# A fused attention and two-MoE kernel: the first MoE2 weight splits let go one per step, row-list merges queued later, and eight softplus copies moved to ScalarE

## The chip, the cores and the metric

The kernel runs on one core of a Trainium2 chip. The metric is the device time of one execution in microseconds (us). Five engines run side by side, each through its own list of instructions in order: TensorE (PE in the rows; PEld is its weight load), VectorE (DVE), ScalarE (ACT), GpSimd (POOL) and SyncE (SP), which issues most DMAs. An instruction that waits holds up everything behind it on its engine. TensorE's granted clock has two levels here, 1.2 and 2.4 GHz; in the rows it stands as a share of the full level (PEclk).

## What is computed

```python
attn_out = _attn_ref(q, k, v)                  # 4 x 8 heads, 576 tokens, window 128, head_dim 64
x = attn_out.transpose(0, 2, 1, 3).reshape(2304, 512)
# MoE1: one dense block with a softplus between
h = x @ w_in                                   # 512 -> 2048
g = np.maximum(h, 0.0) + np.log1p(np.exp(-np.abs(h)))
x = g @ w_out                                  # 2048 -> 512
# MoE2: 8 experts, the best two for each token
noisy_logits = x @ w_gate + np.log1p(np.exp(x @ w_noise)) * noise
top2 = np.argpartition(-noisy_logits, 2, axis=1)[:, :2]
top2_w = softmax(noisy_logits at top2)
for e in range(8):
    for k in range(2):
        mask = top2[:, k] == e
        h = np.maximum(x[mask] @ w1[e], 0.0)
        out[mask] += top2_w[mask, k, None] * (h @ w2[e])
```

## The kernel before

The 2304 tokens are cut into 9 chunks of 256 (`NCH`). Three stages follow each other and overlap at their borders.

**Attention** fills the first chunks. **MoE1** runs as a list of 144 jobs (`jobs`, `NT` = 144); job t is a chunk c and one sixteenth fc of the hidden width. The loop at the end of the kernel does, for each t: `mm1(t)`, the up matmuls of job t (12 matmuls into a PSUM buffer `h`), some side work, `mm2(t - 3)`, the down matmuls of the job three steps before (6 matmuls into `y`), and some side work again. There are two `h` buffers, so `mm1(t)` can only start when VectorE has read the `h` of job t - 2. I call the last jobs NT-8 to NT-1, and one turn of this loop a step.

Between `mm1` and `mm2` a job passes through the softplus chain: ScalarE takes Abs, Exp and Ln (L584 to L586, tiles `sa`, `sl`), VectorE takes `su` (L592) and `sl` (L587, the one that reads `h` and lets its buffer go), GpSimd adds a rounding correction in halves of 128 columns (L559, `su` and `sl`), and then `gh`, a rounded copy, is made (ScalarE L589 for the first six sixteenths of a chunk, VectorE L590 for the others) and `gl`, the rest (VectorE L591).

When a chunk of MoE1 is complete, `route(c)` is fed into the side work, one item in each half step: transposes of the chunk (L679 evacuates them, `x1T`), the logits (L687), `r_sum` and `r_top2` (the small VectorE operations of L723), then `r_rank(c)`, whose TensorE matmuls need `r_mb`, the mask of the chosen experts, and which ends with four indirect DMAs of GpSimd (L790) that write token records into lists by expert (`rect`). Behind the last chunk comes `late_table`, whose matmul needs `mcum`, the running count.

**MoE2** works on groups of 256 or 128 list entries. For each group SyncE reads the four record lists (`rk`, L1074); `merge` (VectorE, L1085 and L1088) folds them into `rc`; GpSimd then gathers the rows (L1102, `xg`); TensorE transposes them, and `xh`, `xl` are made (L1120, L1121). Groups 0 to 3 are known early (an early table made from the first six chunks), so group 0 is merged and gathered while MoE1 still runs.

The MoE2 weights come as tiles of 128 x 1024 (0.5 MB): `w2_load` issues the load on SyncE, into four tiles of their own (`raw` in the rows) or into the ring of 24 weight tiles (`rawp`), and `w2_split` queues the split, `whi` on ScalarE (L1212) and `wlo` on VectorE (L1210), which lets a `raw` tile go. At most `NSPLIT` = 5 split tiles stand ahead of their use. In the kernel before no split is queued until the flag `splitting` is set at t == NT - 4; then `pump` queues all five.

The order on each engine is made by the class `Order`, when the program is built: each operation has an estimated cost, `chain(..., after=x)` puts a chain of operations into a heap x us of planned time from now, and the operations are written out in the order of their planned start. The numbers in the plan set the order alone; on the chip semaphores set the time.

Of the kernel before, what the change touches and what calls it, by code (L numbers as in the profile page):

```python
# [14 lines left out]
AF = mybir.ActivationFunctionType  # L15
# [8 lines left out]
class Order:  # L24
# [11 lines left out]
    def chain(self, *steps, after=0.0):  # L36

        heapq.heappush(self.heap, (self.now + after, self.count, steps, 0))
        self.count += 1
# [54 lines left out]
def ca(n):  # L94
    return 0.16 + n * 0.00083
# [15 lines left out]
def moe_chain_kernel(ctx, tc, qk, v, w_in, w_out, w_gate, w_noise, noise, w1, w2, out):  # L111
# [6 lines left out]
    NF = w_in.shape[0]  # L118
# [442 lines left out]
    def mm1(t):  # L561
        c, fc = divmod(t, NF)
        if c == 0:
            weights(2 * fc)
        if fc == 0:
            u = attn_last(c)
            for hp in range(4):
                need(("c", 4 * u + hp))
            for z, x in enumerate(XT[c]):
                dma(lambda z=z, x=x: SP.dma_start(xspill[c, z], f32(x).rearrange("p k t -> p (k t)")),  # L570
                    ("xo", c, z), 1 << 19)
        if fc == NA:
            for z in range(2):
                need(("xi", c, z))
            if c + 1 < NCH:
                x_load(c + 1)
        w = W[2 * fc]
        ph = up(lambda z, kc: w[:, z, kc * P:(kc + 1) * P], XT[c], CT, ("hr", t))
        a = tl(mid, [P, CT], F32, "sa", 2, ("g", t))
        u = tl(mid, [P, CT], F32, "su", 3, ("g", t))  # L580
        l = tl(mid, [P, CT], F32, "sl", 3, ("g", t))
        gh = tl(mid, [P, CT], F32R, "gh", 4, ("mm2", t))
        gl = tl(mid, [P, CT], F32R, "gl", 4, ("mm2", t))
        chain(("A", ca(CT), lambda: ACT.activation(a, ph, AF.Abs)),  # L584
              ("A", ca(CT), lambda: ACT.activation(a, a, AF.Exp, scale=-1.0), ("e", t)),
              ("A", ca(CT), lambda: ACT.activation(l, a, AF.Ln, bias=1.0)),  # L586
              ("V", cv(CT), lambda: DVE.scalar_tensor_tensor(l, ph, 0.0, l, op0=OP.max, op1=OP.add), ("hr", t)),  # L587
              ("P", cg(CT), lambda: by_halves(l, l, u, OP.add), None, (("d", t),)),
              ("A", ca(CT), lambda: ACT.activation(gh, l, AF.Copy)) if fc < NA else  # L589
              ("V", cv2(CT), lambda: DVE.tensor_copy(gh, l)),  # L590
              ("V", cv(CT), lambda: DVE.tensor_sub(gl, l, f32(gh)), ("g", t)))  # L591
        chain(("V", cv2(CT), lambda: DVE.tensor_scalar(u, a, 1.0, 1.0, op0=OP.add, op1=OP.subtract), None, (("e", t),)),  # L592
              ("P", cg(CT), lambda: by_halves(u, a, u, OP.subtract), ("d", t)), after=2 * ca(CT) + 0.15)
        if fc == NA - 1:
            for z in range(2):
                emitted(("xo", c, z))
            mark(("mm1", c))
        if fc == NF - 1:
            mark(("mm1b", c))
        G[t] = (gh, gl)  # L600
# [195 lines left out]
    def route(c):  # L796
        for _ in range(3):
            yield None
        yield lambda: r_transpose(c, 0)
        yield lambda: r_transpose(c, 1)  # L800
        if c + 1 < NCH:
            yield lambda: part_load(c + 1)
        yield lambda: r_logits(c)
        yield None
        yield None
        yield lambda: r_sum(c)
        for _ in range(6):
            yield None
        yield lambda: r_rank(c)
        if c == NCH - 1:  # L810
            yield None
            yield lambda: late_table(c)

    nconv, nfreed, nback = [0], [0], [0]
# [246 lines left out]
    def g_rows(g):  # L1061

        n, eo, i = groups[g]
        eo = TB[eo]
        rc = tl(p2, [P, 2, 2], I32, "rc", 6, ("gdone", g))
        rk = tl(p2, [P, NCOPY, 2, 2], I32, "rk", 6, ("rows", g))
        GR[g] = dict(rc=rc)
        ps = pieces(g)
        r0 = {}

        def read(k, i, dst, m):
            if i not in r0:
                r0[i] = SP.value_load(eo[0:1, 1, i:i + 1], min_val=0, max_val=E * T)
            SP.dma_start(dst, rect[k][bass.ds(r0[i], dst.shape[1] * m), :].rearrange("(a p) z -> p a z", p=m))  # L1074

        for i, sl in ps:
            m = sl.stop - sl.start
            for k in range(NCOPY):
                reads.append((g, lambda k=k, i=i, sl=sl, m=m: read(k, i, rk[sl, k, :n, :], m)))
                if sl.start:  # L1080
                    reads.append((g, lambda k=k, i=i, m=m: read(k, i, rk[:m, k, 1:2, :], m)))

        def merge():

            DVE.tensor_reduce(rc[:, :n, 0], rk[:, :, :n, 0].rearrange("p k a -> p a k"), axis=AX.X, op=OP.min)  # L1085
            if n == 1:
                DVE.tensor_reduce(rc[:P // 2, 1:, 0], rk[:P // 2, :, 1:, 0].rearrange("p k a -> p a k"), axis=AX.X, op=OP.min)
            DVE.tensor_reduce(f32(rc[:, :n, 1]), f32(rk[:, :, :n, 1]).rearrange("p k a -> p a k"), axis=AX.X, op=OP.add)  # L1088
        def last():
            chain(("V", 0.4, merge, ("rows", g)), after=6.0)  # L1090
            if g < 3 or g - 3 in turned:
                g_start(g)
            GR[g]["read"] = True
        reads.append((g, last))
# [38 lines left out]
    REG, W2, RAW2 = {}, {}, {}  # L1133
    NSPLIT = 5
    NXTRA = 4
    splitting = [False]
    extra, inring, nsplit = set(), [0], [0]

    def ring_left():
# [59 lines left out]
    def w2_split():  # L1199
        skip_singles()  # L1200
        j = wsp[0]
        if j >= wl[0] or not splitting[0] or nsplit[0] >= NSPLIT or nback[0] < len(sidx) or ring_left() < 2:
            return False
        wsp[0] += 1
        nsplit[0] += 1
        t = RAW2[j]
        hi, lo = W2[j] = [wpool.tile([P, 1024], F32R, name=x, tag="w", bufs=NRING) for x in ("whi", "wlo")]

        def low():
            DVE.tensor_sub(lo, t, f32(hi))  # L1210
            w2_drop(j)
        chain(("A", ca(1024), lambda: ACT.activation(hi, t, AF.Copy), None, (("r2", j),)),  # L1212
              ("V", cv(1024), low, ("w2", j)))
        return True
# [216 lines left out]
    for t in range(NT + max(L2, len(items) + 2)):  # L1431
        if t == 4:
            SP.dma_start(wgn[:, :, :E], w_gate.rearrange("(c p) e -> p c e", p=P))
            SP.dma_start(wgn[:, :, E:2 * E], w_noise.rearrange("(c p) e -> p c e", p=P))
            SP.dma_start(nz, noise.rearrange("(a p) e -> p a e", p=P))
        if t == 20:
            prepare1()
        if t > 40 and t % 2:
            p = next(zfeed, None)
            if p is not None:  # L1440
                p()
        due[0] = min(NSL, 2 * NA + max(0, t - 2 * NA + 2) // 2)
        if t in starts:
            c, n = starts[t]
            if feed is not None:
                for p in feed:
                    p()
            feed = pieces_of(c) if c + 1 < NCH else None
            total = 2 * (attn_until(c + 1) - attn_until(c)) if feed else 0
            fed, gap, gaps = 0, 0, 2 * n - 2  # L1450
        if t == last_start - (NF - NA):
            open_p2()
        if t == last_start - (NF - NA) + 2:
            early_table(NCH - 4)
        if t == last_start:
            few_t()
        if t == NT - 4:
            splitting[0] = True
            pump()
        if t < NT:  # L1460
            c, fc = jobs[t]
            if c == NCH - 1 and fc == 1:
                x_load(0)
            mm1(c * NF + fc)
            if c == 0 and fc == NA + 3:
                part_load(0)
            used(2 * fc, c)
            if NT - 3 < t:
                if t == NT - 2:
                    read_rows(0)  # L1470
                    need(("gl", 0))
                g_transpose(0, t - NT + 2)
                if t == NT - 1:
                    turned.add(0)
                    if "read" in GR.get(3, ()):
                        g_start(3)
        else:
            phase2(t - NT)
        side_work()
        if 0 <= t - L2 < NT:  # L1480
            c, fc = jobs[t - L2]
            mm2(c * NF + fc)
            used(2 * fc + 1, c)
            if fc == NA - 1:
                part_evac(c)
            if fc == NF - 1:
                y_evac(c)
                rfeed = chained(rfeed, route(c))
        if 0 <= t - NT - 2 < len(items):
            s3(*items[t - NT - 2])  # L1490
        side_work()
# [65 lines left out]
```

## Time and profile before

| | us |
|---|---|
| median of 3 runs | 1101.99 |
| the profiled execution | 1101.02 |
| its span, first to last instruction | 1098.9 |
| TensorE matmul busy | 1040.1 (95%) |
| VectorE busy | 703.8 (64%) |
| ScalarE busy | 608.2 (55%) |
| GpSimd busy | 582.4 (53%) |

TensorE is busy nearly all the time, and its shares hide two kinds of lost time: where it is idle, and where it is busy at the lower clock. The change lies around the border of MoE1 and MoE2, from about 573 to 660 us of the span, so what matters is read from that stretch.

### The profile page before, as it was taken

What the parts mean: (1) busy time and instruction counts of PE and PEld (TensorE: products, weight loads), DVE (VectorE), ACT (ScalarE), POOL (GpSimd) and SP (SyncE); (2) the same over time, 40 slices, a digit from 0 to 9 for tenths busy, and PEclk for the clock granted to TensorE, in tenths of its full rate; (3) what the DMA queues carried; (4) which work ended last, traced back from release to release, by engine and by line L of the source; (5) the groups of instructions that cost most, each with busy time, mean ns of one, the idle gap of its engine ahead of it and who ended that gap; (6) DMA issues with size and microseconds to landing.
All of it is one profiled execution on the core that took longest, in us unless ns stands there. A gap on an engine that the chain in (4) does not pass through costs nothing.

```text
span 1098.9 us, 21433 instructions
## 1 busy us (share of the span) xinstructions
PE 1040.1 (95%) x7045; PEld 881.7 (80%) x7045; DVE 703.8 (64%) x1910; ACT 608.2 (55%) x1447; POOL 582.4 (53%) x935
## 2 busy tenths in 40 slices
PE   5699999999999999999988899999999999999995
PEld 3577777777789888888877789999996999689964
DVE  7965778888764666666766577665553655365531
ACT  7976778888664444444435345555543554355431
POOL 4776779989786677777766233332222231323111
PEclk8899999999999999999999899999999999999998
DMA  7331453565683322122238759878889987897742
GB/s 296 133 117 50 167 195 130 191 231 170 196 311 119 123 78 77 42 75 78 87 105 257 275 139 253 261 216 214 229 224 330 315 231 219 314 325 233 204 116 31
DMA packets 97317, 202.13 MB, mean 184 GB/s; under 512 B 34160, under 2 KB 44912, under 8 KB 97200
## 3 DMA queue, kind: packets, MB, share of 16 engines
q1 hardware_dynamic: 87264, 180.21, 49.4%
q0 software_dynamic: 9936, 20.49, 9.4%
q8 instruction: 58, 0.95, 0.4%
q14 instruction: 59, 0.48, 0.2%
HBM read 161.49 MB, written 39.17 MB: 183 GB/s over the span
## 4 chain that ended last, share of the span: by engine, by line
PE 66%; DVE 3%; POOL 3%; DMA 3%; ACT 2%; issue 2%; SPq 1%; DVEq 0%; POOLq 0%; ACTq 0%
PE h L189 30%; PE y L189 19%; PE z L189 10%; PE t L200 3%; DMA rk<-rect 2%; PE h L1281 2%; PE y L1331 1%; PE t L189 1%; POOL sl L559 1%; POOL su L559 1%; PE z L1331 1%; PE t L342 1%; DMA out<-ys,rc 1%; POOL s L375 1%; DVE wlo L1210 0%
## 5 line engine op out<-in xcount | busy, mean ns | idle before, releaser
L189 PE MATMUL h<-xh,w 128*128 128x256 f32 x1152 | 240.5, 292 | 8.4 <-DVE sl L587 8.4
L1344 POOL DMA_INDIRECT out<-ys,rc x42 | 82.6, 1967 | 275.4 <-DVE ys L1354 116.1
L189 PEld LDWEIGHTS h<-xh,w 128*128 128x128 f32 x1152 | 191.8, 194 | 23.4 <-DVE sl L587 11.7
L1210 DVE TENSOR_TENSOR wlo<-rawp,whi 128x1024 fp32r<-128x1024 f32 x111 | 135.5, 1221 | 96.2 <-ACT whi L1212 94.2
L1212 ACT ACTIVATE whi<-rawp 128x1024 fp32r<-128x1024 f32 x111 | 117.5, 1060 | 124.6 <-PE h L189 91.5
L189 PE MATMUL y<-w,gh 128*128 128x512 f32 x552 | 179.8, 407 | 0.0
L559 POOL TENSOR_TENSOR su<-sa,su 128x128 f32<-128x128 f32 x288 | 134.6, 488 | 75.4 <-DVE su L592 62.9
L189 PE MATMUL h<-xl,w 128*128 128x256 f32 x576 | 164.7, 286 | 1.0 <-DVE xl L439 1.0
L189 PE MATMUL h<-xh,whi 128*128 128x256 f32 x576 | 164.6, 286 | 0.6 <-DVE gl L1269 0.6
L189 PE MATMUL h<-xl,whi 128*128 128x256 f32 x576 | 164.1, 285 | 0.6 <-issue 0.6
L189 PE MATMUL h<-xh,wlo 128*128 128x256 f32 x576 | 164.1, 285 | 0.0
L559 POOL TENSOR_TENSOR sl<-sl,su 128x128 f32<-128x128 f32 x288 | 135.6, 492 | 7.2 <-DVE sl L587 5.9
L584 ACT ACTIVATE sa<-h 128x256 f32<-128x256 f32 x144 | 54.8, 381 | 143.0 <-PE h L189 89.8
L189 PEld LDWEIGHTS h<-xh,whi 128*128 128x128 f32 x576 | 111.1, 193 | 11.9 <-issue 3.2
L189 PEld LDWEIGHTS h<-xl,whi 128*128 128x128 f32 x576 | 111.1, 193 | 6.1 <-issue 0.8
L189 PEld LDWEIGHTS h<-xl,w 128*128 128x128 f32 x576 | 111.6, 194 | 4.1 <-DVE xl L439 1.3
L189 PEld LDWEIGHTS h<-xh,wlo 128*128 128x128 f32 x576 | 111.1, 193 | 0.0
L189 PE MATMUL y<-w,gl 128*128 128x512 f32 x276 | 108.8, 394 | 0.0
L189 PEld LDWEIGHTS y<-w,gh 128*128 128x128 f32 x552 | 95.5, 192 | 16.3 <-issue 2.4
L375 POOL TENSOR_TENSOR s<-s,st 128x256 f32<-128x256 f32 (+2 forms) x144 | 91.9, 660 | 29.1 <-DVE st L366 13.4
L1102 POOL DMA_INDIRECT xg<-x1buf,rc x39 | 46.0, 1180 | 83.5 <-PE h L1281 26.2
L360 ACT ACTIVATE s<-s,st 128x256 f32<-128x256 f32 (+2 forms) x160 | 76.0, 478 | 17.7 <-DVE st L354 17.6
(265 smaller groups left out, 2172.0 us busy)
## 6 DMA issues: line engine op xcount, KB each, us to landing
rawp<-in_moe_w SPq DMA_DIRECT2D x147, 512.0 KB
raw<-in_moe_w SPq DMA_DIRECT2D x45, 512.0 KB
qkT<-in_qk SPq DMA_DIRECT2D x20, 512.0 KB
raw<-in_moe_w_in SPq DMA_DIRECT2D x16, 512.0 KB
raw<-in_moe_w_out SPq DMA_DIRECT2D x16, 512.0 KB
out<-zero SPq DMA_DIRECT2D x19, 256.0 KB
xspill<-xh SPq DMA_DIRECT2D x9, 512.0 KB
xspill<-xl SPq DMA_DIRECT2D x9, 512.0 KB
```

The lines of the kernel that those rows point to most:

```text
L189: PE.matmul(o, l, r, start=start, stop=stop)
L200: PE.transpose(o, i, idn)
L360: ACT.activation(s[:nq, j, :n], s[:nq, j, :n], AF.Exp, bias=st[:nq, 0, y], scale=-1.0, accum_out=sums[:nq, y, 0])
L375: POOL.tensor_tensor(s[:nq, j, :n], s[:nq, j, :n], st[:nq, 3, 2 * x + j:2 * x + j + 1].to_broadcast([nq, n]), OP.mult)
L559: POOL.tensor_tensor(o[:, z], x[:, z], y[:, z], op)
L584: chain(("A", ca(CT), lambda: ACT.activation(a, ph, AF.Abs)), ("A", ca(CT), lambda: ACT.activation(a, a, AF.Exp, scale=-1.0), ("e", t)), ( ...
L1102: POOL.indirect_dma_start(out=x, out_offset=None, in_=x1buf[:T - 3 * CT if g < NEARLY else TPAD, :], in_offset=bass.IndirectOffsetOnAxis(a ...
L1210: DVE.tensor_sub(lo, t, f32(hi))
L1212: chain(("A", ca(1024), lambda: ACT.activation(hi, t, AF.Copy), None, (("r2", j),)), ("V", cv(1024), low, ("w2", j)))
L1281: PE.matmul(ph[sl, x * 256:(x + 1) * 256], GR[g]["xT"][:, kc, sl], RAW2[j][:, kc * 256:(kc + 1) * 256], start=kc == 0, stop=kc == KC - 1)
L1331: PE.matmul(Y2[g][0][sl], th[:, x, sl], RAW2[j][:, x % 2 * 512:x % 2 * 512 + 512], start=ff == 0, stop=ff == NF1 - 1)
L1344: POOL.indirect_dma_start(out=out[:, :], out_offset=bass.IndirectOffsetOnAxis(ap=rc[:sl.stop - sl.start, a + x, 0:1], axis=0), in_=ys[sl], ...
```

## The change

Five edits:

- **Splits.** The flag is replaced by a count: at t = NT-7 and at each step behind it one more split may be queued, up to five. The first five splits so stand in steps NT-7 to NT-3, one in each.
- **gh.** For the last eight jobs of MoE1 `gh` is made on ScalarE and not on VectorE.
- **Merges.** The chain with `merge` of a group is put 12 us into planned time (group 1), 24 us (groups 2 and 3) or 12 us (later groups), where 6 us stood for all. Group 0 keeps 6.
- **Rank.** `r_rank` of the last chunk but one comes two items (one step) later.
- **Late table.** `late_table` comes two items (one step) later.

```diff
-              ("A", ca(CT), lambda: ACT.activation(gh, l, AF.Copy)) if fc < NA else
+              ("A", ca(CT), lambda: ACT.activation(gh, l, AF.Copy)) if fc < NA or t >= NF * NCH - 8 else
               ("V", cv2(CT), lambda: DVE.tensor_copy(gh, l)),
...
-        for _ in range(6):
+        for _ in range(8 if c == NCH - 2 else 6):
             yield None
         yield lambda: r_rank(c)
         if c == NCH - 1:
-            yield None
+            for _ in range(3):
+                yield None
             yield lambda: late_table(c)
...
-            chain(("V", 0.4, merge, ("rows", g)), after=6.0)
+            chain(("V", 0.4, merge, ("rows", g)), after=6.0 if g == 0 else 12.0 if g < 2 else 24.0 if g < 4 else 12.0)
...
-    splitting = [False]
+    most = [0]
...
-        if j >= wl[0] or not splitting[0] or nsplit[0] >= NSPLIT or nback[0] < len(sidx) or ring_left() < 2:
+        if j >= wl[0] or nsplit[0] >= min(NSPLIT, most[0]) or nback[0] < len(sidx) or ring_left() < 2:
             return False
...
-        if t == NT - 4:
-            splitting[0] = True
+        if t >= NT - 7:
+            most[0] += 1
             pump()
```

ScalarE in the steps before the end of MoE1, the kernel before (`lgp` evacuates the logits, `sa<-h` begins the softplus of a job):

```order
L691 ACTIVATE lgp<-t 128x256
L1212 ACTIVATE whi<-raw_7759 128x1024
L1212 ACTIVATE whi<-raw_7771 128x1024
L1212 ACTIVATE whi<-raw_7774 128x1024
L1212 ACTIVATE whi<-raw_7777 128x1024
L584 ACTIVATE sa<-h 128x256
L1212 ACTIVATE whi<-rawp 128x1024
L584 ACTIVATE sa<-h 128x256
```

The same engine with the change, two steps earlier, from the second split on:

```order
L1213 ACTIVATE whi<-raw_7771 128x1024
L589 ACTIVATE gh<-sl 128x256
L584 ACTIVATE sa<-h 128x256
L679 ACTIVATE x1T<-t 128x4x128
L585 ACTIVATE sa<-sa 128x256
L586 ACTIVATE sl<-sa 128x256
L589 ACTIVATE gh<-sl 128x256
L679 ACTIVATE x1T<-t 128x4x128
L1213 ACTIVATE whi<-raw_7774 128x1024
L584 ACTIVATE sa<-h 128x256
```

The four `whi` that stood in a row, ahead of two waiting `sa<-h`, now have a step of softplus work between them, and each step's list also holds a `gh<-sl`, which waits for GpSimd.

VectorE at the same place, the kernel before:

```order
L590 CAST gh<-sl 128x256
L1210 TENSOR_TENSOR wlo<-raw_7759,whi 128x1024
L591 TENSOR_TENSOR gl<-sl,gh 128x256
L1210 TENSOR_TENSOR wlo<-raw_7771,whi 128x1024
L1210 TENSOR_TENSOR wlo<-raw_7774,whi 128x1024
L700 TENSOR_REDUCE lg<-t 128x32
L1210 TENSOR_TENSOR wlo<-raw_7777,whi 128x1024
L1210 TENSOR_TENSOR wlo<-rawp,whi 128x1024
L592 TENSOR_SCALAR su<-sa 128x256 x2
L723 TENSOR_SCALAR r_u<-r_a 128x16
L587 SCALAR_TENSOR_TENSOR sl<-h,sl 128x256 x2
```

VectorE with the change, from the last `gh` that it makes:

```order
L590 CAST gh<-sl 128x256
L1211 TENSOR_TENSOR wlo<-raw_7759,whi 128x1024
L591 TENSOR_TENSOR gl<-sl,gh 128x256
L592 TENSOR_SCALAR su<-sa 128x256
L587 SCALAR_TENSOR_TENSOR sl<-h,sl 128x256
L1211 TENSOR_TENSOR wlo<-raw_7771,whi 128x1024
L591 TENSOR_TENSOR gl<-sl,gh 128x256
L592 TENSOR_SCALAR su<-sa 128x256
L587 SCALAR_TENSOR_TENSOR sl<-h,sl 128x256
L591 TENSOR_TENSOR gl<-sl,gh 128x256
L1211 TENSOR_TENSOR wlo<-raw_7774,whi 128x1024
```

All five `wlo` stood between one `gh` and the next two `sl<-h`; now one `sl<-h` follows each of them.

VectorE somewhat later, where `r_mb` is made for the rank of the last chunk but one, the kernel before (`rc<-rk` is the merge of group 3):

```order
L723 MAX_INDEX r_i_8417<-r_v_8416,r_n 128x8 x2
L723 TENSOR_TENSOR r_g<-r_v_8416 128x2
L723 CAST r_ix<-r_i_8417 128x4
L1269 SCALAR_TENSOR_TENSOR gl<-h,gh 128x256
L723 TENSOR_TENSOR r_m_8419<-iot,r_ix 128x16
L1085 TENSOR_REDUCE rc<-rk 128x2
L1088 TENSOR_REDUCE rc<-rk 128x2
L723 TENSOR_TENSOR r_m_8419<-iot,r_ix 128x16
L590 CAST gh<-sl 128x256
L723 TENSOR_TENSOR r_mb<-r_m_8419 128x16
```

The same with the change:

```order
L723 TENSOR_TENSOR r_g<-r_v_8444 128x2
L723 CAST r_ix<-r_i_8445 128x4
L1270 SCALAR_TENSOR_TENSOR gl<-h,gh 128x256
L723 TENSOR_TENSOR r_m_8447<-iot,r_ix 128x16 x2
L723 TENSOR_TENSOR r_mb<-r_m_8447 128x16
L723 COPY rec<-tok 128x2 x2
L591 TENSOR_TENSOR gl<-sl,gh 128x256
```

The merge is gone from the path to `r_mb`; the merges of groups 2 and 3 now stand behind the rank, and that of group 1 ahead of the second `xl` of group 0.

## Rows read from the trace of the kernel before

**Rows 1.** Stretches: us, busy us of PE, PEld, DVE, ACT, POOL (count), PEclk, DMA share, GB/s.
```profile
560.00:589.00 29.00, 28.66 (x189) 24.85 (x189) 20.98 (x69) 16.05 (x35) 20.36 (x41) 0.99 0.38 96
589.00:621.00 32.00, 23.80 (x130) 20.69 (x129) 19.56 (x64) 7.98 (x22) 16.57 (x26) 0.84 0.89 312
645.00:654.00 9.00, 6.88 (x37) 6.15 (x36) 5.66 (x20) 4.07 (x6) 4.00 (x3) 0.81 0.50 99
```

**Rows 2.** TensorE's waits, whole span: what waited, releaser, us, times, longest.
```profile
PE h L189 <- DVE sl L587: 8.4, 5, 4.5
PE t L189 <- DVE r_mb L723: 3.4, 2, 3.1
PE t L189 <- DVE mcum L776: 3.1, 2, 2.1
PE h L189 <- DVE gl L1269: 0.6, 1, 0.6
```

**Rows 3.** Timeline of TensorE: start, us, instruction, in brackets idle before it.
```profile
556.79 0.39 PE L189 MATMUL h<-xh,w 128*128 128x256 f32 x1 [3.02 <-DVE sl L587]
...
573.38 0.28 PE L189 MATMUL h<-xh,w 128*128 128x256 f32 x1
...
576.20 0.28 PE L189 MATMUL h<-xh,w 128*128 128x256 f32 x1
...
594.06 0.38 PE L189 MATMUL h<-xh,w 128*128 128x256 f32 x1 [4.54 <-DVE sl L587]
...
608.99 0.19 PE L189 MATMUL t<-r_mb,tri 128*128 128x8 bf16 x1 [3.11 <-DVE r_mb L723]
...
648.15 0.18 PE L189 MATMUL t<-mcum,ones 128*128 128x8 bf16 x1 [2.12 <-DVE mcum L776]
```

**Rows 4.** Stretches behind three of the waits: us, PE busy (count), PEclk, DMA share, GB/s.
```profile
594.00:598.50 4.50, 4.44 (x21) 0.62 0.99 327
...
609.00:613.00 4.00, 4.00 (x20) 0.50 1.04 412
613.00:617.00 4.00, 4.00 (x20) 0.74 0.76 255
...
648.00:653.00 5.00, 4.85 (x21) 0.66 0.19 34
```

**Rows 5.** Timeline of ScalarE at the splits.
```profile
583.80 3.89 ACT L1212 ACTIVATE whi<-raw 128x1024 fp32r<-128x1024 f32 x4
587.60 0.37 ACT L584 ACTIVATE sa<-h 128x256 f32<-128x256 f32 x1
```

**Rows 6.** Timeline of VectorE, from the splits to the rank.
```profile
588.09 2.35 DVE L1210 TENSOR_TENSOR wlo<-raw,whi 128x1024 fp32r<-128x1024 f32 x2
...
593.60 0.74 DVE L587 SCALAR_TENSOR_TENSOR sl<-h,sl 128x256 f32<-128x256 f32 x2
...
599.96 0.17 DVE L1085 TENSOR_REDUCE rc<-rk 128x2 int32<-128x8 int32 x1 [2.97 <-DMA rk<-rect]
...
603.78 2.30 DVE L723 TENSOR_TENSOR r_g<-r_v 128x2 f32<-128x2 f32 x1
...
608.32 0.17 DVE L1085 TENSOR_REDUCE rc<-rk 128x2 int32<-128x8 int32 x1 [1.76 <-DMA rk<-rect]
```

**Rows 7.** Groups of ScalarE, 330 to 600 us: busy us, mean ns, idle before.
```profile
L586 ACT ACTIVATE sl<-sa 128x256 f32<-128x256 f32 x85 | 35.5, 418 | 2.4
...
L584 ACT ACTIVATE sa<-h 128x256 f32<-128x256 f32 x85 | 32.6, 384 | 123.0 <-PE h L189 73.7 <-POOL sl L559 17.6 <-POOL su L559 7.8
L679 ACT ACTIVATE x1T<-t 128x512 f32<-128x512 f32 x16 | 9.6, 599 | 3.9 <-PE t L200 3.9
```

**Rows 8.** Timeline of GpSimd.
```profile
578.37 1.02 POOL L790 DMA_INDIRECT rect<-rec,pi  x1 [0.17 <-issue]
...
604.35 1.70 POOL L559 TENSOR_TENSOR sl<-sl,su 128x128 f32<-128x128 f32 x4
```

**Rows 9.** Group of VectorE, 330 to 600 us: the small operation of Rows 6.
```profile
L723 DVE TENSOR_TENSOR r_g<-r_v 128x2 f32<-128x2 f32 x7 | 1.0, 143 | 0.0
```

## The prediction, made before the changed kernel was run

> **What bounds the kernel now.** I read the stretches first [rows 1], then TensorE's waits [rows 2], then its timeline at the waits [rows 3]. TensorE is the bound: from 560 to 589 us it is busy 28.66 of 29 us at a granted clock of 0.99. Time is to be had only where it is idle or runs at the lower level, and that is around the border of the two MoEs: from 589 to 621 us it is busy 23.80 of 32 us with the clock at 0.84 on average, and from 645 to 654 us 6.88 of 9 us at 0.81. The reader should see in [rows 3] three long waits there: 4.54 us for `sl` (L587), 3.11 us for `r_mb`, 2.12 us for `mcum`. A fourth, 3.02 us at 556.79, lies before any row that the change moves, and stays.
>
> Behind each wait the clock is low for a while [rows 4]. I price that as stretch length times the missing share: 4.5 x 0.38 = 1.7 us behind the first, 4 x 0.50 + 4 x 0.26 = 3.0 us behind the second, 5 x 0.34 = 1.7 us behind the third. Together 6.4 us, beside 4.54 + 3.11 + 2.12 = 9.8 us of idle time. So 16.2 us is the most that this stretch can give, if the clock stays at its full level where no wait precedes, as it does at 0.99 in [rows 1].
>
> **Splits, one per step.** In the kernel before four `whi` take ScalarE from 583.80 for 3.89 us [rows 5], 0.97 us each. The Abs of the next job, behind them in the list, starts only at 587.60. Then VectorE runs its `wlo`, 2.35 us for two [rows 6], 1.18 us each, and comes to the two `sl` that let both `h` buffers go only at 593.60. That is the 4.54 us.
>
> With the change one `whi` and one `wlo` stand in each of five steps. Does a step hold them? A step is 2.82 us (573.38 to 576.20 [rows 3]). ScalarE has Abs 0.38, Exp about 0.42, Ln 0.42 [rows 7], one `gh`, which I take at 0.38 as an operation of the same size, and `whi` 0.97: 2.57 us of 2.82. It fits, with a quarter of a us to spare. Two evacuations `x1T` of 0.60 us each [rows 7] fall into the same steps, so ScalarE runs about 1 us late for two or three steps. What TensorE allows: `mm1(t)` needs the `sl` of job t - 2, so from the end of one `mm1` to the start of the next but one there are a whole step and one `mm2`, about half a step: 2.82 + 1.4 = 4.2 us. The shortest chain in it is Abs, Exp, Ln and `sl` (0.74 us for two [rows 6]): 0.38 + 0.42 + 0.42 + 0.37 = 1.6 us, some 1.9 with hand-overs. The cover is 2.3 us in each step. One `whi` ahead of the Abs takes 0.97 of it, one `wlo` ahead of the `sl` 1.18: 2.15 us, if both meet one job at the worst place. So I expect this wait to go, and put 1.0 us of new short waits against it: two splits at their worst place plus the late `x1T` leave the cover short by some tenths in two or three steps. The bounds are 0 us (all covered) and 5 x (1.70 + 1.18) = 14.4 us (each `wlo` waits for four GpSimd halves, 1.70 us [rows 8], and then holds its engine). I take a value near the lower end, since each step has the cover anew and the order puts only one split into it.
>
> **gh on ScalarE.** VectorE loses eight small copies, ScalarE gains eight. What matters is the queue: a `gh` waits for GpSimd's `sl`, and behind it on ScalarE now stands the next job's Abs, Exp or Ln, or an `x1T` on which the logits matmul waits. On VectorE the same wait stood ahead of `sl`. I count it at nothing but what is in the 1.0 us above; if GpSimd is late, each us comes through to TensorE after 2.3 us of cover.
>
> **Merges queued later.** On VectorE, merges wait for the row lists 2.97 us at 599.96 and 1.76 us at 608.32 [rows 6]; behind the second stands `r_mb`, on which TensorE waits 3.11 us. In the new order the merges of groups 2 and 3 stand behind the rank. The gathers of these groups on GpSimd follow the scatter DMAs of the rank now. Their cover: a group takes TensorE eight steps, 8 x 2.82 = 22.6 us, and group 2 is transposed in the second half of group 1, so a few us cost nothing; without that cover each us would be one. Group 1's merge stands ahead of the second `xl` of group 0; its reads on SyncE stand behind two loads that wait for the first and second `wlo`, but those now come some 10 us earlier. Price 0; bounds 0 and 3 us (the 2.97 us again). For later groups the merges wait less; a 0.6 us wait for `gl` in [rows 2] stands behind such a merge, and I count it as won.
>
> **Rank and late table.** The rank comes one step, 2.82 us, later, and what made `r_mb` late is gone: the two merge waits above, and one small operation that took 2.30 us [rows 6], where its group takes 0.14 on average [rows 9]. So 3.11 us go, and the 3.0 of clock; bounds for what is left 0 and 3.11 + 3.0. The late table comes 2.82 us later, against a wait of 2.12: 0.7 us to spare, so 2.1 + 1.7 us go. Behind it the list of later groups is known some 2.8 + 1.7 = 4.5 us later as measured in TensorE's work (its own step, and the clock loss that no longer slows TensorE meanwhile); the first of these groups starts after four groups of 22.6 us, so their weights have tens of us of lead.
>
> **The sum.** 16.2 + 0.6 - 1.0 = 15.8 us. From the profiled execution, 1101.02, that is 1085.2; the median of the runs lies 1.0 us above it, so 1086.
>
> **What one rule of the skill would make of it.** The small operation of 2.30 us began under GpSimd's four halves (604.35 for 1.70 us [rows 8]) and ended as they did: VectorE waited for GpSimd. The Trainium skill, page "SBUF — State Buffer", section "Who interferes with whom", says that a VectorE instruction with two inputs in SBUF contends with a GpSimd instruction that reads SBUF, and that the loser blocks fully. `wlo` has two such inputs. By that rule this row is what each interleaved `wlo` can meet, where all five stood in GpSimd's idle time before; it is the first rival below.
>
> **The rivals.**
>
> *GpSimd falls behind.* For five steps the four halves (1.70 us) and a `wlo` (1.18) would exclude each other: 2.88 us of 2.82, and two scatter DMAs of 1.02 us [rows 8] fall into the same steps. GpSimd would be late by 5 x 0.06 + 2 x 1.02 = 2.3 us, `gh` with it, and with ScalarE's own 1 us that passes the cover of 2.3 by about 1; a wait of 3 us in all with its clock loss of 1.7 replaces my 1.0: 3.7 us more, 1090. For it speaks the 2.30 us row, against it that the halves are short and the cover is renewed. Chance 0.17.
>
> *The rank still waits.* If `r_mb` stays behind a merge or a GpSimd burst, 3.1 + 3.0 us are not won: 1092. Against it: no merge stands ahead of it in the new order. Chance 0.08.
>
> *Slower.* Every `wlo` meets a full burst: 14.4 us, and five low-clock stretches of 1.7 us, 8.5, make 22.9 us of new loss against 16.8 won: 1101.0 + 6.1 + 1.0 = 1108. It decides from 3.4 us for each split, where gain and loss are equal. Against it: 4.2 us between the two `mm1` would have to be used up five times. Chance 0.05.
>
> *It doesn't do what it says.* The clock loss or the waits reappear a few us later, at `xl` of group 0 or at the first weights, and little moves: 1097 to 1102. Chance 0.10.
>
> **How the numbers follow.** The forecast has 0.60, with its own range 1083.5 (no new wait at all, and a little more) to 1088.5 (half of a rank-sized loss). With the first two rivals, up to 1093, that holds 0.8. About 0.5%, 5.5 us, is what a measurement of this kernel can tell from no change. Faster by more than that: 0.60 + 0.17 + 0.08 = 0.85; within: 0.10; slower: 0.05.
>
> **What would show it.** In the changed profile: no wait of `h` for `sl` (L587) over 2 us between 573 and 600; the rank's matmul without a wait; the late table's without a wait; the clock at 0.95 or more from 560 to 650; the MoE2 part beginning some 6 us earlier, near 596. Wrong would be: waits of TensorE for `x1T` or `sl` at the logits or in the last jobs, with GpSimd busy throughout and `wlo` over 2 us; or `xl` of group 0 waiting for the merge of group 1.

## The result, and the profile after

| | us |
|---|---|
| before, median of 4 runs beside it | 1103.26 (1101.97 to 1106.5) |
| changed kernel, median of 4 runs | 1085.65 (1084.62 to 1087.03) |
| ratio, 95% interval | 0.9841 [0.9821, 0.986] |
| profiled execution, before and after | 1101.02 and 1087.03 |
| its span, before and after | 1098.9 and 1085.3 |

The change wins 17.6 us by the medians. The two profiled executions differ by 14.0 us only: the one of before lies below all four runs of its kernel, the one of after is the longest of its four. What follows is read from these two and explains 13.6 us of span.

The first lines of the page of the changed kernel (busy us, share of the span and instructions of each engine; then two rows of the 40 slices):

```profile
PE 1036.2 (95%) x7045; PEld 878.0 (81%) x7045; DVE 702.9 (65%) x1902; ACT 609.6 (56%) x1455; POOL 587.1 (54%) x935
...
PE   5799999999999999999989999999999999999995
...
PEclk8799999999999999999999999999999999999998
```

The shares of the engines hardly move (TensorE 95% before and after), so they can't show where 13.6 us went. The waits can. TensorE's waits in the changed kernel (what waited, releaser, us in total, times, longest), beside [rows 2]:

```profile
PE h L189 <- DVE sl L587: 4.4, 6, 2.8
...
PE t L687 <- ACT x1T L679: 1.1, 1, 1.1
PE t L189 <- DVE mcum L776: 1.0, 1, 1.0
...
PE t L189 <- DVE r_mb L723: 0.3, 1, 0.3
```

`sl` falls from 8.4 us to 4.4, `r_mb` from 3.4 to 0.3, `mcum` from 3.1 to 1.0, and the 0.6 us for `gl` is gone. One wait is new: 1.1 us of the logits (L687) for `x1T`. TensorE's timeline of the changed kernel, beside [rows 3], shows where they stand (idle before, in brackets):

```profile
558.06 0.38 PE L189 MATMUL h<-xh,w 128*128 128x256 f32 x1 [2.77 <-DVE sl L587]
...
585.22 0.64 PE L687 MATMUL t<-x1T,wgn 128*32 128x256 f32 x8 [1.08 <-ACT x1T L679]
...
592.25 0.39 PE L189 MATMUL h<-xh,w 128*128 128x256 f32 x1 [0.32 <-DVE sl L587]
...
596.14 0.38 PE L189 MATMUL h<-xh,w 128*128 128x256 f32 x1 [0.45 <-DVE sl L587]
...
599.43 0.28 PE L189 MATMUL h<-xh,whi 128*128 128x256 f32 x1
...
605.40 0.18 PE L189 MATMUL t<-r_mb,tri 128*128 128x8 bf16 x1
...
611.24 0.46 PE L200 MATMUL t<-ident_r,xg 128*128 128x128 f32 x4
...
639.67 0.18 PE L189 MATMUL t<-mcum,ones 128*128 128x8 bf16 x1
...
812.59 2.16 PE L1282 MATMUL h<-rawp,xs 128*64 128x256 f32 x17
```

The rank (605.40) and the late table (639.67) start without a wait. Three marks in the timeline of the kernel before are needed to measure the gain: the first MoE2 matmul, the first transpose of group 1, and the first matmul on `xs`, far behind; each is the same matmul of TensorE's list in both kernels:

```profile
602.02 0.35 PE L189 MATMUL h<-xh,whi 128*128 128x256 f32 x1
...
620.32 0.45 PE L200 MATMUL t<-ident_r,xg 128*128 128x128 f32 x4
...
825.39 3.67 PE L1281 MATMUL h<-rawp,xs 128*64 128x256 f32 x32
```

So the 13.6 us go as follows. At group 0's merge, ahead of the changed stretch, this execution is 1.27 us late (558.06 against 556.79). At group 1's transposes it is 620.32 - 611.24 = 9.08 us early: the border won 10.35. At `xs` it is 12.80 us early: the late table won 3.72. The last 0.8 comes behind that.

The stretches of the changed kernel (us, busy us of PE, PEld, DVE, ACT, POOL, then PEclk, DMA share and GB/s), beside [rows 1, 4]:

```profile
558.00:562.00 4.00, 3.94 (x16) 3.67 (x17) 3.38 (x5) 2.16 (x8) 3.67 (x8) 0.57 0.44 131
575.00:584.00 9.00, 9.00 (x61) 7.97 (x59) 7.08 (x12) 4.80 (x10) 8.58 (x13) 1.00 0.67 138
584.00:589.00 5.00, 3.92 (x30) 3.11 (x30) 3.82 (x6) 4.67 (x11) 2.90 (x8) 1.00 0.86 255
589.00:621.00 32.00, 31.16 (x210) 26.91 (x210) 23.02 (x65) 16.73 (x39) 18.73 (x26) 1.00 1.01 337
645.00:654.00 9.00, 9.00 (x61) 8.23 (x60) 6.97 (x20) 3.05 (x5) 4.34 (x3) 1.00 0.50 78
```

From 589 to 621 us TensorE is busy 31.16 us of 32 at the full level (2.4 GHz), where it was busy 23.80 at 0.84 on average. The 1.08 us of idle time near 585 left the clock at 1.00. What is still lost at the lower clock lies ahead of it: behind the 2.77 us wait at 558 the clock is 0.57 for four us. In the stretch itself the short waits are left, 1.08 + 0.32 + 0.45 = 1.85 us.

### The profile page after: what moved, and what is told of

Its sections match the earlier page's. It is cut to its first block, busy times and chain, and to the rows that moved or that the text cites. A ratio compares the mean times of both kernels' runs of the same rounds, so it can differ in the third digit from the quotient of the medians.

```text
span 1085.3 us, 21420 instructions
## 1 busy us (share of the span) xinstructions
PE 1036.2 (95%) x7045; PEld 878.0 (81%) x7045; DVE 702.9 (65%) x1902; ACT 609.6 (56%) x1455; POOL 587.1 (54%) x935
## 4 chain that ended last, share of the span: by engine, by line
PE 66%; POOL 4%; DVE 4%; DMA 2%; issue 2%; ACT 2%; SPq 0%; POOLq 0%; DVEq 0%; ACTq 0%
PE h L189 30%; PE y L189 18%; PE z L189 10%; PE t L200 2%; PE h L1282 2%; PE y L1332 1%; POOL sl L559 1%; POOL su L559 1%; PE t L189 1%; DMA rk<-rect 1%; PE z L1332 1%; DMA rect<-rec,pi 1%; PE t L342 1%; DVE su L592 1%; POOL s L375 1%
## 5 line engine op out<-in xcount | busy, mean ns | idle before, releaser
L1211 DVE TENSOR_TENSOR wlo<-rawp,whi 128x1024 fp32r<-128x1024 f32 x109 | 133.2, 1223 | 109.5 <-ACT whi L1213 99.1
L1213 ACT ACTIVATE whi<-rawp 128x1024 fp32r<-128x1024 f32 x109 | 115.3, 1060 | 115.0 <-PE h L189 82.6
L559 POOL TENSOR_TENSOR sl<-sl,su 128x128 f32<-128x128 f32 x288 | 138.5, 501 | 7.8 <-DVE sl L587 6.3
L591 DVE TENSOR_TENSOR gl<-sl,gh 128x256 fp32r<-128x256 f32 x144 | 71.2, 494 | 22.9 <-ACT gh L589 20.6
```

Of the source, the lines that this page charges most:

```text
L559: POOL.tensor_tensor(o[:, z], x[:, z], y[:, z], op)
```

## Where the new wait comes from

GpSimd and ScalarE in the changed kernel, ahead of the logits at 585.22, and one `wlo` of VectorE (three timelines, GpSimd first):

```profile
577.56 1.78 POOL L790 DMA_INDIRECT rect<-rec,pi  x1 [0.16 <-issue]
579.37 1.87 POOL L559 TENSOR_TENSOR sl<-sl,su 128x128 f32<-128x128 f32 x2
...
583.37 0.86 POOL L559 TENSOR_TENSOR sl<-sl,su 128x128 f32<-128x128 f32 x2
```

```profile
581.28 0.42 ACT L589 ACTIVATE gh<-sl 128x256 fp32r<-128x256 f32 x1 [2.72 <-POOL sl L559]
...
584.27 0.42 ACT L589 ACTIVATE gh<-sl 128x256 fp32r<-128x256 f32 x1 [1.06 <-POOL sl L559]
584.59 0.58 ACT L679 ACTIVATE x1T<-t 128x512 f32<-128x512 f32 x1
```

```profile
579.69 1.25 DVE L1211 TENSOR_TENSOR wlo<-raw,whi 128x1024 fp32r<-128x1024 f32 x1
```

Two things meet. A pair of GpSimd halves takes 1.87 us where a `wlo` lies beside it (VectorE runs this one from 579.69 for 1.25 us) and 0.86 where none does; a scatter takes 1.78 beside another `wlo` (577.00, 1.48 us) and 0.98 without. So `sl` is late. And `gh`, now on ScalarE, waits for it with the `x1T` of the logits in line behind.

## The experiments

The theory going in: each edit takes away the wait that the prediction gave it. The rivals: a wait only moves to the next instruction that shares the cause, and the moved operations (interleaved `wlo`, `gh` on ScalarE) cost something of their own. First each edit alone, on the kernel before; its runs beside these four had a median of 1102.6 us.

**The splits alone.**

```diff
-    splitting = [False]
+    most = [0]
...
-        if t == NT - 4:
-            splitting[0] = True
+        if t >= NT - 7:
+            most[0] += 1
             pump()
```

> The kernel before with the split edit alone. My theory, that each edit removes its own wait: the 4.5 us wait for sl and the 1.7 us of low clock behind it go, 1 to 2 us of new short waits come, the 3.1 us wait for r_mb with its 3.0 us of clock loss stays and so does the one for mcum (2.1 + 1.7): 1096 to 1099 us against 1102. Rival, that the merges waiting on VectorE are the one cause behind all of it: the freed time only shifts the wait to the next merge, 1101 to 1103 us.

Measured: 1102.97 us, ratio 0.9991 [0.9971, 1.001]. No change. The 4.54 us wait is down to 0.28, and yet nothing is won. VectorE and TensorE of this kernel at the rank (two timelines):

```profile
605.45 0.17 DVE L1085 TENSOR_REDUCE rc<-rk 128x2 int32<-128x8 int32 x1 [3.40 <-DMA rk<-rect]
...
606.60 0.17 DVE L723 TENSOR_TENSOR r_mb<-r_m 128x16 bf16<-128x16 f32 x1
```

```profile
606.83 0.19 PE L189 MATMUL t<-r_mb,tri 128*128 128x8 bf16 x1 [5.41 <-DVE r_mb L723]
```

TensorE comes to the rank 4.5 us earlier (601.42 against 605.88; 0.8 of it was there ahead of the change, at 556), but the second merge (608.32 in [rows 6]) still stands ahead of `r_mb`, and its row lists land only 2.9 us earlier than before. The merge waits 3.40 us where it waited 1.76, and the rank 5.41 where it waited 3.11; two further waits of 1.1 and 1.0 us stand at the first merge. The theory's 1096 to 1099 is wrong: the stall moved on, as the rival had it. (The trace is of the shortest of its ten runs, 1098.81 us; what the others lose beyond it is not shown.)

**The merges alone.**

```diff
-            chain(("V", 0.4, merge, ("rows", g)), after=6.0)
+            chain(("V", 0.4, merge, ("rows", g)), after=6.0 if g == 0 else 12.0 if g < 2 else 24.0 if g < 4 else 12.0)
```

> The kernel before with the later merges alone. My theory: the 2.97 and 1.76 us that VectorE waits for row lists vanish, r_mb is ready some 4 us earlier than TensorE needs it, so 3.1 us of waiting and 3.0 us of clock loss go and nothing else: 1095 to 1097 us; the 4.5 us wait for sl stays. Rival, that r_mb is late because of the GpSimd burst (the 2.30 us operation) and the five wlo ahead of it: r_mb stays late by 2 us or more, 1099 to 1102 us.

Measured: 1095.46 us, 0.9922 [0.9895, 0.995]. As expected: the rank waits 0.45 us, the burst's wait (4.55) and the late table's (2.19) stay.

**Rank and late table alone.**

```diff
-        for _ in range(6):
+        for _ in range(8 if c == NCH - 2 else 6):
             yield None
         yield lambda: r_rank(c)
         if c == NCH - 1:
-            yield None
+            for _ in range(3):
+                yield None
             yield lambda: late_table(c)
```

> The kernel before with the rank and the late table one step later, and nothing else. My theory: the late table loses its 2.1 us wait and 1.7 us of clock loss; the rank comes 2.8 us later against a wait of 3.1, so 0.3 us is left and the clock stays up: 3.8 + 5.8 = 9.6 us, 1091 to 1094 us. Rival, that the work put ahead of the rank waits itself behind the same merge (its gl stands behind it on VectorE): only the late table's 3.8 us are won, 1097 to 1099 us.

Measured: 1095.37 us, 0.9932 [0.9914, 0.995]. Less than expected, and between theory and rival. The rank no longer waits, but the merge does, and the next in line pays. VectorE, then TensorE:

```profile
610.23 0.17 DVE L1086 TENSOR_REDUCE rc<-rk 128x2 int32<-128x8 int32 x1 [2.43 <-DMA rk<-rect]
```

```profile
610.81 1.06 PE L189 MATMUL y<-w,gh 128*128 128x512 f32 x2 [2.16 <-DVE gh L590]
```

**gh alone.**

```diff
-              ("A", ca(CT), lambda: ACT.activation(gh, l, AF.Copy)) if fc < NA else
+              ("A", ca(CT), lambda: ACT.activation(gh, l, AF.Copy)) if fc < NA or t >= NF * NCH - 8 else
```

> The kernel before with gh of the last eight jobs on ScalarE, and nothing else. My theory: no change, 1101 to 1104 us, since the copies lie beside other work on either engine and the burst of five splits still holds both. Rival, that VectorE's wait for GpSimd ahead of sl is a cause of the 4.5 us wait: 3 us or more are won, 1099 us or less.

Measured: 1097.95 us, 0.9955 [0.9941, 0.997]. I had expected nothing. The time is the rival's, but its cause is not: the burst's wait falls only from 4.54 to 3.96. The rest comes from the rank, which doesn't wait. In this kernel `r_mb` has run on VectorE ahead of the second merge:

```profile
604.45 0.32 DVE L723 TENSOR_TENSOR r_mb<-r_m 128x16 bf16<-128x16 f32 x1
...
608.26 0.17 DVE L1085 TENSOR_REDUCE rc<-rk 128x2 int32<-128x8 int32 x1 [2.66 <-DMA rk<-rect]
```

Eight copies fewer on VectorE changed who stands behind that merge. Now it is `gl` (a TensorE wait of 1.13 us), and behind the merge of a later group, which waits 3.89 us at 664.59, `gl` again (1.87 us).

The four gains alone (0, 7.1, 7.2 and 4.7 us by the medians) say little of what each is worth in the whole, since three of them take away the same wait. So each was taken out of the changed kernel; the kernel before had a median of 1101.37 beside these.

**All but the splits.**

```diff
-        if t >= NT - 7:
-            most[0] += 1
+        if t == NT - 4:
+            splitting[0] = True
             pump()
```

> The changed kernel with the splits let go in one burst again, all else as changed. My theory: the 4.5 us wait for sl returns with its 1.7 us of clock loss, the short waits of the one-per-step order (1.9 us) go: 1089 to 1091 us against 1085.7. Rival, that the later merges and gh on ScalarE have made the burst harmless: 1087 us or less.

Measured: 1090.17 us, 0.9895 [0.986, 0.993], as expected. TensorE's timeline has the wait back, and from 592 to 598 us the clock is 0.72:

```profile
592.67 0.54 PE L189 MATMUL h<-xh,w 128*128 128x256 f32 x1 [3.95 <-DVE sl L587]
```

In the company of the other edits the splits are worth 4.5 us, alone nothing.

**All but gh.**

```diff
-              ... if fc < NA or t >= NF * NCH - 8 else
+              ... if fc < NA else
```

> The changed kernel with gh of the last eight jobs on VectorE again. My theory: the 1.1 us wait of the logits for x1T goes, since it comes from gh waiting for GpSimd ahead of x1T on ScalarE; VectorE waits for GpSimd ahead of sl instead, some tenths each: 1084 to 1087 us. Rival, that gh alone won 5 us over the kernel before because VectorE is freed, and does so here too: 1089 us or more.

Measured: 1085.86 us, 0.9848 [0.9814, 0.9882], the same as with it. The `x1T` wait is gone. GpSimd and ScalarE ahead of the logits (two timelines):

```profile
578.21 1.78 POOL L790 DMA_INDIRECT rect<-rec,pi  x1 [0.16 <-issue]
580.02 0.89 POOL L559 TENSOR_TENSOR sl<-sl,su 128x128 f32<-128x128 f32 x2
```

```profile
582.01 0.60 ACT L679 ACTIVATE x1T<-t 128x512 f32<-128x512 f32 x1 [0.48 <-PE t L200]
```

`x1T` now waits for TensorE's transposes alone, and the logits don't wait. But this kernel doesn't tell the two causes apart: the scatter is as long as before (1.78), while the pair ahead of `x1T` is not (0.89 for 1.87), since with `gh` on VectorE the second `wlo` starts only at 581.15, behind that pair. Pairs that do meet a `wlo` later, at 585.23 and 588.76, take 1.90 and 1.86. In exchange two small waits (0.48 and 0.38 us) stand at the first MoE2 matmuls.

**All but the merges.**

```diff
-            chain(..., after=6.0 if g == 0 else 12.0 if g < 2 else 24.0 if g < 4 else 12.0)
+            chain(..., after=6.0)
```

> The changed kernel with all merges at 6 us again. My theory: VectorE again waits for row lists ahead of r_mb and of xl; the rank's later place covers 2.8 us of it, 2 to 3 us stay and keep their clock loss: 1089 to 1092 us. Rival, that the later rank already covers the wait in full: 1085 to 1087 us.

Measured: 1093.77 us, 0.9936 [0.9914, 0.9957], somewhat more lost than expected. Now it is a merge ahead of the second `xl` of group 0, that of group 2 (group 1's has run at 590.55 without a wait; VectorE, then TensorE):

```profile
600.17 0.17 DVE L1086 TENSOR_REDUCE rc<-rk 128x2 int32<-128x8 int32 x1 [3.41 <-DMA rk<-rect]
...
601.22 0.67 DVE L1122 TENSOR_TENSOR xl<-t,xh 128x512 fp32r<-128x512 f32 x1
```

```profile
600.89 0.36 PE L189 MATMUL h<-xh,whi 128*128 128x256 f32 x1 [3.31 <-DVE r_n L723]
```

A second merge, of a later group, waits 3.47 us at 664.85 and costs TensorE 1.50 for `gl`.

**All but rank and late table.**

```diff
-        for _ in range(8 if c == NCH - 2 else 6):
+        for _ in range(6):
...
-            for _ in range(3):
-                yield None
+            yield None
```

> The changed kernel with the rank and the late table at their old places. My theory: the late table's 2.1 us and 1.7 us of clock return, and the rank waits just under 1 us (r_mb is ready at 603.4, TensorE would be there at 602.6): 1089.5 to 1091.5 us. Rival, that the other edits make mcum early as well: 1086 to 1087 us.

Measured: 1091.94 us, 0.9907 [0.9873, 0.9941], a little beyond the range expected. The rank waits 0.71 us and the late table 2.19:

```profile
637.47 0.18 PE L189 MATMUL t<-mcum,ones 128*128 128x8 bf16 x1 [2.19 <-DVE mcum L776]
```

So in the whole the merges are worth 8.1 us, rank and late table 6.3, the splits 4.5 and gh 0.2, by the medians. These differences set medians of these four kernels against that of the changed kernel, 1085.65, which was measured beside other runs of the kernel before (1103.26 there, 1101.37 here). By the ratios to the kernel before they are 10.5, 7.3, 5.9 and 0.8 us: the order holds, the sizes do so only within some 2.5 us, and the interval of the splits' ratio touches that of the changed kernel (both have 0.986).

By then one pattern stood behind most of the waits: a merge waits for its row lists, and whatever is next on VectorE pays. The wait of 2.77 us at 558, which I had set aside, has the same shape: group 0's merge, in the trace of the changed kernel, waits 5.78 us for `rk` ahead of that `sl`:

```profile
556.90 0.17 DVE L1086 TENSOR_REDUCE rc<-rk 128x2 int32<-128x8 int32 x1 [5.78 <-DMA rk<-rect]
```

The last three kernels test this and the GpSimd pairs; the kernel before had 1103.6 us beside them.

**Group 0's merge later as well.**

```diff
-            chain(..., after=6.0 if g == 0 else 12.0 if g < 2 else 24.0 if g < 4 else 12.0)
+            chain(..., after=12.0 if g < 2 else 24.0 if g < 4 else 12.0)
```

> The changed kernel with one number more: group 0's merge is queued 12 us into planned time too, where 6 us stood. In every kernel so far TensorE waits 2.3 to 3.0 us near 556 to 559 us for sl (L587); in the trace of the changed kernel VectorE's list before that sl holds group 0's merge, which waits for its row lists. Theory: the merge is the cause, so the 2.77 us wait goes, with about 1 to 2 us of low clock behind it, and nothing else is late: 1081 to 1083 us, against 1085.65. Rival 1: the wait has another cause (the softplus chain at the start of MoE1's last third), and the time stays within 1 us of 1085.65. Rival 2: group 0's gather, a step or two later, makes MoE2's first xh late, and the gain is lost there: 1085 to 1088 with a wait of 2 us or more near 597.

Measured: 1081.2 us (1080.36 to 1083.24, 5 runs), 0.9803 [0.9789, 0.9816]: as the theory said, and better than both kernels (the changed kernel's interval begins at 0.9821). The merge runs without waiting, and TensorE is busy 20 of 20 us at the full clock (VectorE's timeline, then the stretch):

```profile
555.69 0.15 DVE L1086 TENSOR_REDUCE rc<-rk 128x2 int32<-128x8 int32 x1
```

```profile
540.00:560.00 20.00, 20.00 (x133) 17.49 (x133) 14.68 (x57) 10.00 (x27) 14.13 (x29) 1.00 0.56 177
```

**The same without gh.** The edit is that of the run above and the one of "all but gh" together.

```diff
-              ... if fc < NA or t >= NF * NCH - 8 else
+              ... if fc < NA else
...
-            chain(..., after=6.0 if g == 0 else 12.0 if g < 2 else 24.0 if g < 4 else 12.0)
+            chain(..., after=12.0 if g < 2 else 24.0 if g < 4 else 12.0)
```

> The same without the gh edit: the last softplus copies stay on VectorE. Theory: as leaving gh out of the changed kernel moved the time by 0.2 us only, this lands within 1 us of the kernel with group 0's merge late and gh on ScalarE, 1081 to 1083; the 1.08 us wait for x1T near 585 is absent. Rival: gh on ScalarE is what gives VectorE the room for the merge in its new place, and this kernel is 2 us or more slower than the one with both.

Measured: 1081.11 us (1079.53 to 1081.68, 5 runs), 0.9791 [0.9777, 0.9804]. The same as with it: gh on ScalarE can be left out.

**wlo in quarters.**

```diff
-            DVE.tensor_sub(lo, t, f32(hi))
+            if most[0] <= 7 and j <= 8:
+                for i in range(4):
+                    s = slice(256 * i, 256 * i + 256)
+                    DVE.tensor_sub(lo[:, s], t[:, s], f32(hi[:, s]))
+            else:
+                DVE.tensor_sub(lo, t, f32(hi))
```

> The changed kernel, each of the first five wlo written as four subtractions of 256 columns in the same place of the order, where one of 1024 stood. In the changed kernel GpSimd's pairs of halves (L559, sl) take 1.86 to 1.91 us where a wlo lies beside them and 0.86 to 0.88 where none does, and one scatter 1.78 for 0.98. Theory: the two engines take turns by whole instructions, so a half waits for at most one quarter: the stretched pairs fall to 1.2 to 1.5 us, the scatter to 1.0 to 1.3, and TensorE's wait for x1T of 1.08 near 585 shrinks by half or more; time 1083.5 to 1086. Rival: the same bytes slow GpSimd down by sharing, whatever their grouping, and pairs stay at 1.8 to 1.9 with the scatter at 1.8 and the time at 1085 to 1087.

Measured: 1086.38 us, 0.984 [0.9825, 0.9855]. GpSimd, then VectorE:

```profile
577.92 0.99 POOL L790 DMA_INDIRECT rect<-rec,pi  x1 [0.16 <-issue]
578.94 1.07 POOL L559 TENSOR_TENSOR sl<-sl,su 128x128 f32<-128x128 f32 x2
...
582.24 1.23 POOL L559 TENSOR_TENSOR sl<-sl,su 128x128 f32<-128x128 f32 x2
```

```profile
577.37 2.33 DVE L1214 TENSOR_TENSOR wlo<-raw,whi 128x256 fp32r<-128x256 f32 x4
...
580.76 2.40 DVE L1214 TENSOR_TENSOR wlo<-raw,whi 128x256 fp32r<-128x256 f32 x4
```

The pairs fall from 1.9 to 1.07 to 1.24 us, the scatter from 1.78 to 0.99, and the `x1T` wait is gone, with `gh` still on ScalarE: the stretch is a cause of that wait. The rival, that equal bytes slow GpSimd equally, falls with that. The Trainium skill, page "SBUF — State Buffer", section "Who interferes with whom", says that only the port pair that VectorE and GpSimd share causes contention between them, "and it's an exclusive lock"; the trace agrees, since the stretch shrinks with the length of the instruction. But the time doesn't move: the four quarters take 1.70 to 2.40 us where one `wlo` took 1.23 to 1.48, and a `sl` wait of 0.92 us stands at the end of MoE1. The theory's claim on the time (1083.5 to 1086) was not met.

## Why the prediction was right, step by step

- **The sum.** It said 15.8 us, from the profiled execution of 1101.02 to 1085.2, and 1.0 more to the median: 1086. The median is 1085.65. Trace against trace the gain is 14.0, so that close a hit is partly luck: 1.27 us of the difference lie ahead of the change, the profiled execution of after is 1.4 us above its own median, and that of before was not 1.0 but 2.2 us below the median of the runs beside it.
- **The border** (waits of 4.54 and 3.11, their clock 1.7 and 3.0, less 1.0) was put at 11.35 and came to 10.35. The mis-sized term is the 1.0 for new short waits: they are 1.08 + 0.32 + 0.45 = 1.85. The clock terms hold, since no stretch from 575 to 660 is below 1.00.
- **Late table:** 2.1 + 1.7 = 3.8 predicted, 3.72 measured. **The `gl` wait** of 0.6 is gone; what comes behind `xs` is 0.8.
- **"GpSimd falls behind"** was put as a rival, and its mechanism is there: interleaved `wlo` stretch GpSimd's halves, `gh` is late, and TensorE waits for `x1T`. It was priced at 3 us with 1.7 of clock; the new waits are 1.85 us and the clock didn't fall. That row of 2.30 us [rows 6] was a good warning and a poor price. I also read it a little wrong: the operation began at 603.78, ahead of the halves that I named (604.35 [rows 8]), under the `su` halves before them.
- **gh at nothing:** right in the whole (0.2 us with all else in place; with group 0's merge late it is 0.1 the other way), wrong alone (4.7 us). I looked at ScalarE's queue and not at what VectorE's order becomes with eight operations fewer.
- **Merges at price 0**, with the rank's term put down to the two merge waits: the cause was right. But I gave the 6.1 us to the rank's paragraph, as though delaying the rank were what wins it. Moving the merges alone leaves the rank a wait of 0.45 us; leaving the merges in place costs 8.1 us, and delaying the rank alone hands the wait to `gh`. The bound of 3 us that I put on a merge ahead of the second `xl` of group 0 turned up where the edit was left out (3.31 us), though with group 2's merge and not group 1's.
- **The splits:** 4.54 + 1.7 - 1.0 = 5.2 us predicted; 4.5 in the whole. That they need the other edits to be worth anything was the last rival ("the waits reappear a few us later"), and it is true of the splits alone.
- **MoE2's beginning "some 6 us earlier"** is the step that failed: 599.43 against 602.02 is 2.6 us, 3.9 without the 1.27. My own terms ahead of that mark are 4.54 + 1.7 - 1.0 = 5.2, and with the real new waits 4.4. The rest of the border is won behind it: from there to group 1's transposes it was 18.30 us and is 11.81.
- **"Stays"** for the 3.02 us wait at 556.79: right for this change. It has the same cause as those it removes, and one more number wins it.

What stays open is what fills the time of a row-list read. How long it is, SyncE's timelines show. Its reads come in fours, and the last of group 3 is issued here, in the kernel before and with the splits alone:

```profile
600.40 0.38 SPq L1074 DMA_DIRECT2D rk<-rect  x1
```

```profile
597.09 0.38 SPq L1074 DMA_DIRECT2D rk<-rect  x1
```

The merges that wait for them run 7.9 and 8.4 us behind (608.32 and 605.45). For group 0 in the kernel before it is 5.6 us (550.04 to 555.63). The plan put each merge 6 us behind its reads. With the splits alone the read is issued 3.3 us earlier, where TensorE comes 4.5 us earlier, and the time behind the issue doesn't shrink. Why that time is 5.6 us in one place and 8.4 in another was not tried.

## What to carry to other kernels

When one instruction waits on a transfer in an in-order list, the wait belongs to that instruction, and the victim is whoever stands next: removing an earlier stall (the splits alone) or moving the victim (the rank alone) handed it to the next in line here, moving the waiting instruction ended it. Look for every place where the same instruction waits, since the same edit may win there too (here 4.5 us more). And judge an edit by taking it out of the finished set as well as by adding it alone: here one was worth 0 alone and 4.5 in company, another 4.7 alone and 0.2 in company.

## What the runs showed of the hardware

- One VectorE subtraction of 128x1024 with both inputs in SBUF delays a pair of GpSimd halves by about 1.0 us (0.86 to 1.87) and a scatter's issue by 0.8 (0.98 to 1.78). Cut into four, it delays them by 0.2 to 0.4 and by nothing that shows, but then takes up to 2.40 us itself. I had expected the halves to be delayed, not the scatter.
- The other way round VectorE did not come in between two halves at the rank. The 128x2 operation of 2.30 us [rows 6] lay under `su` halves and the four `sl` halves behind them [rows 8], and ended with the last (606.08 against 606.05). With rank and late table alone it is the same, 2.30 us from 605.01, with halves up to 607.29. GpSimd, the kernel before:

```profile
602.62 1.77 POOL L559 TENSOR_TENSOR su<-sa,su 128x128 f32<-128x128 f32 x4
```

- The granted clock stayed at 1.00 behind an idle time of 1.08 us near 585 (changed kernel). It was 0.57 behind 2.77 us at 558 in the same execution, and 0.50 from 606.5 to 611 us, at the end of 5.41 us and behind it (splits alone).
- A wait of that middle length did not always cost the clock. At the same place TensorE waited 2.89 us with rank and late table alone, 2.66 without the splits and 2.87 without gh, and in those three executions the clock stayed at 1.00; TensorE then ran into a second wait for `sl`, of about 1.4 us. Without gh (TensorE, then the stretch):

```profile
558.69 0.39 PE L189 MATMUL h<-xh,w 128*128 128x256 f32 x1 [2.87 <-DVE sl L587]
...
563.18 0.39 PE L189 MATMUL h<-xh,w 128*128 128x256 f32 x1 [1.40 <-DVE sl L587]
```

```profile
558.70:562.70 4.00, 3.08 (x18) 2.48 (x18) 3.38 (x4) 2.29 (x8) 3.67 (x8) 1.00 0.45 131
```

So a clock term behind a wait, as the prediction sums it, is not a loss that stands by itself: here an execution paid either four us at 0.57 (1.7 us) or the second wait (1.4 us).
